# The last block of phase one multiplied plainly, attention work begun in the bursts, and more places for side work in the plain slices

## Chip, cores and metric

One Trainium2 chip, one of its cores. The metric is device time in microseconds (us) of one launch, lower is better. The engines are named as in the profile: PE (TensorE matmul), PEld (its weight loads), DVE (VectorE), ACT (ScalarE), POOL (GpSimd), SP (SyncE, which here only issues DMAs).

## What is computed

```python
# q, k, v: [8, 8, 576, 64]; attention inside chunks of 64 positions
scores = scale * np.matmul(q_c, k_c.transpose(0, 1, 2, 4, 3))
scores = scores - np.max(scores, axis=-1, keepdims=True)
attn = np.exp(scores)
attn = attn / (np.sum(attn, axis=-1, keepdims=True) + 1e-09)
x = (attn @ v_c) as [4608, 512]
x = ((x @ w_a) * (x @ w_b)) @ w_out             # phase one, d_ff 1536
h = ((x @ w1) * (x @ w2)) @ w3                  # phase two, d_ff 1024
out = h @ w_out2                                # [4608, 512]
```

The weights arrive as 64-bit floats and are turned into 32-bit ones on the chip. Each 32-bit operand of a large product is split into a high part and a remainder, and a product is three matmul passes (`SEQ`: high by low, low by high, high by high).

## The kernel before

The 4608 tokens are 9 blocks of 512. A phase (`ph` 0 or 1) goes through the `d_ff` columns in steps `f` of 128 (12 in phase one, 8 in phase two). In a step two first products `a` and `b` are made, multiplied into `g`, and `g` enters the second product, which sums over the steps in four PSUM tiles (`Second`, tiles `acc`, 3 matmuls to a part, 4 parts to a step).

Stages of a phase, in order:

- **Plain slices** (`plain_step`): blocks 0 and 1. Each step has a slice T=0 and a slice T=1; a slice is `first` twice, 12 matmuls each into `pa` and `pb`. The slices of T=0 run `AHEAD` (3) steps ahead of T=1. Only T=0 carries on to its second product; T=1 stores its `g` in the tiles `G`. Meanwhile weights are converted (`Pump`, `Conv`: about four DVE instructions, one of ACT and one of POOL for each) and, in phase one, the attention of the next blocks is computed (`Unit`, one for each block and pair of heads: `turn`, `scores` with `soft1`, `soft2`, `flip`, `apply` with `put`; on PE their tiles are `t`, `s`, `f`, `x`).
- **Burst** (`burst`): second product of the block whose `g` lie in `G`: 12 matmuls for each `f`, first the four parts that were still pending. `ready` makes a step's `gh` (ACT) and `gl` (POOL). The operands of the next two blocks are formed and split meanwhile (`strassen_pieces`: `minus` on DVE, then a cast on ACT and a subtraction on DVE, tiles `xP`).
- **Steps** (`block_steps`, `strassen_step`): two blocks at once by Strassen's scheme, seven products (`product`, tiles `P`) of 6 matmuls with 512 columns, combined by three copies on ACT and three additions on DVE (tiles `c`); `g` of one block goes to its second product, the other waits in `G` for the next burst.
- This pair of burst and steps comes four times in each phase. The fourth has one block alone, the ninth (`LONE`): Strassen inside the block, `single`, with 256 columns to a matmul. In phase one these steps also carry the conversion of the weights `w_out2` and `w3` (26 conversions), transposes of `w3` (`turn_w3`, tile `w3p`, then `w3t`) and eight products `w3 @ w_out2` (`fuse`, 24 matmuls each into `wf`), so that phase two multiplies by one fused matrix.

The order is written by hand (`manual_schedule`): every engine executes its instructions in program order. Side work lies in a `Track`, a list of pieces (cost, starts on PE or not, function). A step calls `point()` at set places; a point emits pieces until the share of cost emitted equals the share of points passed. A piece that starts on PE is emitted only as the first piece of a point (lines 59 to 71), and what is left at the end comes out at once in `finish`:

```python
while self.left and self.done < self.total * self.at / self.points:
    cost, needs, emit = self.left[0]
    if needs and not pe:
        return
```

DMAs of q, k and v are queued by `ask` and put on SP by `tick` (called by `first`, `product` and `Second.part`) or, where a unit needs them, by `settle`. Weight stores are queued by `store` and put on ACT's queue by the second `tick` after it. PSUM has eight banks: `rA` to `rD` for first products and side work, `acc0` to `acc3`. Attention uses `rB` and `rD`, `turn_w3` and `fuse` use `rD`.

Of the kernel before, what the change touches and what calls it, by code (L numbers as in the profile page):

```python
# [9 lines left out]
F32 = mybir.dt.float32  # L10
F32R = mybir.dt.float32r
# [67 lines left out]
def chunk_attention_two_gated_products(  # L79
# [158 lines left out]

    def split(dst_h, dst_l, src, eng_l):
        nc.scalar.copy(dst_h, src)  # L240
        eng_l.tensor_tensor(dst_l, src, dst_h, op=ALU.subtract)  # L241
# [10 lines left out]
    class Unit:  # L252
# [16 lines left out]
        def banks(self, name):  # L269
            return [bank("BD"[i], f"{name}{i}_{self.nm}") for i in range(2)]  # L270
# [149 lines left out]
    class TurnedOnPE(Unit):  # L420
# [47 lines left out]
        def flip_bank(self):  # L468
            return bank("D", f"f_{self.nm}")
# [79 lines left out]
    def strassen_pieces(x32, nm, single=False):  # L549
# [12 lines left out]

        def value(p, kt):
            name = f"x{p}{kt}{nm}"
            if p == "P1":
                return src(0, 0, kt)
            if p == "P2":
                return src(0, 1, kt)
            if p == "P3":
                return src(1, 1, kt)  # L570
            if p == "P5":
                diff["t1", kt] = minus(src(1, 0, kt), src(0, 0, kt), name)
                return diff["t1", kt]
            if p == "P6":
                diff["t2", kt] = minus(src(1, 1, kt), diff["t1", kt], name)
                return diff["t2", kt]
            if p == "P7":
                return minus(src(1, 1, kt), src(1, 0, kt), name)
            return minus(src(0, 1, kt), diff["t2", kt], name)
# [9 lines left out]
        def one(p, kt):  # L589
# [5 lines left out]
        order = ["P5", "P1", "P2", "P6", "P3", "P7", "P4"]  # L595
        return parts, [
            (1.4 if p in ("P5", "P6", "P7", "P4") else 0.7, False, lambda p=p, kt=kt: one(p, kt))
            for p in order
            for kt in range(2)
        ]  # L600

# [87 lines left out]
    def load_part(ph, f, i):  # L689
# [7 lines left out]
        pairs.setdefault((ph, f), {})[i] = t  # L697

# [121 lines left out]
    state = {"pending": None_()}  # L820
# [56 lines left out]
    def plain_step(ph, j, T, f, nm, point, gplaces, sums, tags):  # L877

        w = pairs[ph, f]
        xq = [quadrants[T, 0], quadrants[T, 1]]  # L880
# [11 lines left out]
        first(w, 1, xq, f"pb{nm}", pb)  # L892
        if T == 1:
            nc.vector.tensor_tensor(g_place(ph, f"{ph}p", f, gplaces), pb, sa, op=ALU.mult)
            del pairs[ph, f]
        else:
            nc.vector.tensor_tensor(sa, pb, sa, op=ALU.mult)
            pend.rest()
# [404 lines left out]
```

## Time and profile before

| | before |
|---|---|
| median of 3 runs | 1790.8 us (1788.63 to 1791.69) |
| profiled execution, own time | 1786.45 us |
| its span | 1784.6 us |
| busy share PE / PEld / DVE / ACT / POOL | 90% / 72% / 50% / 31% / 25% |
| granted TensorE clock, mean of the span | 0.963 of 2.4 GHz |

The span runs from the first to the last instruction of the profiled execution. A row of the timeline gives start, length, engine, line, operation, tile written and tiles read, count, and in brackets how long the engine was idle before and what ended that. A row of waits gives the waiting engine and tile, what it waited for, the sum in us, the number of times and the longest. A row of a window gives its length, each engine's busy time and number of instructions, the granted clock, the share of the 16 DMA engines and GB/s.

### The profile page before, as it was taken

The numbers are of one execution on the slowest core, as the hardware profiler recorded it, in microseconds if no ns is written. First come the engines' busy times: TensorE is split into PE (matmuls) and PEld (weight loads), VectorE is DVE, ScalarE is ACT, GpSimd is POOL, SyncE is SP. The second block draws the span as 40 slices with busy tenths as digits, with TensorE's granted clock in tenths as the row PEclk, the third lists the DMA queues.
The fourth block names the chain that finished last, engine by engine and source line by source line (L and its number), as shares of the span: only waits on it lengthen the run. The fifth ranks groups of instructions, "written<-read, shape, count | busy, mean of one in ns | idle before, by whom it ended". The sixth has DMA issues, their size and how long they took to land.

```text
span 1784.6 us, 24867 instructions
## 1 busy us (share of the span) xinstructions
PE 1609.8 (90%) x9232; PEld 1293.8 (72%) x9232; DVE 888.5 (50%) x1484; ACT 557.4 (31%) x1009; POOL 442.7 (25%) x354
## 2 busy tenths in 40 slices
PE   5769999699899999999998798889989989989998
PEld 3557777577677777777886676778768868868787
DVE  5748783476665655555224744355354442242231
ACT  4434443222224222322224322232332331231232
POOL 1304342111123221322123422222122222222232
PEclk8969999899999999999999899999999999999999
DMA  8757766676677887676566876596467756656674
GB/s 212 232 146 227 245 191 197 189 244 198 201 226 223 228 214 204 195 232 192 180 195 226 289 262 217 179 324 212 178 225 257 241 196 216 205 193 205 205 264 174
DMA packets 291703, 385.44 MB, mean 216 GB/s; under 512 B 174848, under 2 KB 195328, under 8 KB 291584
## 3 DMA queue, kind: packets, MB, share of 16 engines
q1 hardware_dynamic: 258656, 298.92, 55.1%
q10 hardware_dynamic: 32928, 84.95, 12.4%
q8 instruction: 73, 1.20, 0.3%
q14 instruction: 46, 0.38, 0.1%
HBM read 301.99 MB, written 81.79 MB: 215 GB/s over the span
## 4 chain that ended last, share of the span: by engine, by line
PE 62%; DVE 14%; DMA 8%; issue 5%; ACT 5%; POOL 2%; SPq 2%; ACTq 1%; POOLq 0%; DVEq 0%
PE P L756 32%; PE acc L785 16%; PE pb L742 5%; PE pa L742 4%; PE wf L988 3%; DVE xP L560 2%; SPq L148 2%; DVE xP L241 2%; DMA wo<-dwo 1%; DVE c L844 1%; ACT xP L240 1%; PE x L391 1%; DMA qk<-in_k_dram 1%; DMA x2d<-ev 1%; ACT ev L794 1%
## 5 line engine op out<-in xcount | busy, mean ns | idle before, releaser
L756 PE MATMUL P<-xP,w 128*128 128x512 f32 (+1 forms) x3360 | 735.8, 372 | 53.4 <-DVE c L844 30.7
L756 PEld LDWEIGHTS P<-xP,w 128*128 128x128 f32 x3360 | 584.3, 192 | 177.5 <-DVE c L844 40.9
L844 DVE TENSOR_TENSOR c<-P,c 128x512 f32<-128x512 f32 (+1 forms) x240 | 148.4, 621 | 350.0 <-PE P L756 338.0
L872 POOL TENSOR_TENSOR G<-c,c 128x512 f32<-128x512 f32 x60 | 78.2, 1303 | 517.0 <-DVE c L844 517.0
L841 ACT COPY c<-P 128x512 f32<-128x512 f32 (+1 forms) x240 | 127.3, 533 | 220.7 <-PE P L756 217.8
L785 PE MATMUL acc<-gh,wo 128*128 128x512 f32 x480 | 174.8, 402 | 0.0
L240 ACT CAST gh<-c 128x512 fp32r<-128x512 f32 x60 | 37.3, 621 | 333.1 <-DVE c L871 323.9
L742 PE MATMUL pb<-xq,w 128*128 128x512 f32 x480 | 124.3, 410 | 0.0
L742 PE MATMUL pa<-xq,w 128*128 128x512 f32 x480 | 121.5, 403 | 1.9 <-DVE w L645 1.9
L241 POOL TENSOR_TENSOR gl<-c,gh 128x512 fp32r<-128x512 f32 x60 | 78.2, 1304 | 162.2 <-ACT gh L240 162.2
L785 PE MATMUL acc<-wo,gh 128*128 128x512 f32 x320 | 112.2, 394 | 3.3 <-ACT gh L240 3.3
L742 PEld LDWEIGHTS pb<-xq,w 128*128 128x128 f32 x480 | 94.2, 199 | 20.9
L742 PEld LDWEIGHTS pa<-xq,w 128*128 128x128 f32 x480 | 91.5, 194 | 22.6 <-DVE w L645 2.3
L785 PEld LDWEIGHTS acc<-gh,wo 128*128 128x128 f32 x480 | 92.3, 192 | 19.9
L871 DVE TENSOR_TENSOR c<-P,c 128x512 f32<-128x512 f32 x60 | 41.5, 691 | 121.2 <-PE P L756 121.2
L785 PE MATMUL acc<-gl,wo 128*128 128x512 f32 x240 | 95.7, 399 | 0.0
L785 PEld LDWEIGHTS acc<-wo,gh 128*128 128x128 f32 x320 | 60.5, 189 | 16.9 <-ACT gh L240 4.1
L240 ACT CAST xP<-xP 128x512 fp32r<-128x512 f32 (+1 forms) x64 | 36.3, 567 | 113.7 <-DVE xP L560 113.7
L195 POOL TENSOR_TENSOR cv<-cv 128x512 f32<-128x512 f32 x38 | 45.3, 1191 | 99.9 <-DVE cv L189 75.0
L241 DVE TENSOR_TENSOR xP<-x,xP 128x512 fp32r<-128x512 f32 (+1 forms) x48 | 49.7, 1080 | 40.7 <-ACT xP L240 40.7
L241 DVE TENSOR_TENSOR xP<-xP,xP 128x512 fp32r<-128x512 f32 (+1 forms) x64 | 44.2, 691 | 43.8 <-ACT xP L240 43.8
L785 PE MATMUL acc<-wo,gl 128*128 128x512 f32 x160 | 63.6, 397 | 1.5 <-POOL gl L241 1.5
(132 smaller groups left out, 2158.8 us busy)
## 6 DMA issues: line engine op xcount, KB each, us to landing
w<-dw SPq DMA_DIRECT2D x200, 512.0 KB, 4.4
wo<-dwo SPq DMA_DIRECT2D x168, 512.0 KB, 4.3
dw<-w ACTq DMA_DIRECT2D x80, 512.0 KB, 4.1
w<-dw SPq DMA_DIRECT2D x80, 256.0 KB, 3.0
su<-d SPq DMA_DIRECT2D x20, 512.0 KB, 5.1
d<-cv ACTq DMA_DIRECT2D x38, 256.0 KB, 4.4
cv_o<-in_moe_w_out_dram SPq DMA_DIRECT2D x18, 512.0 KB, 5.5
x2d<-ev ACTq DMA_DIRECT2D x36, 256.0 KB, 3.6
```

The source lines that it names most:

```text
L148: nc.sync.dma_start(*asks["left"].popleft())
L195: eng.tensor_tensor(self.w, hi.bitcast(F32), lo, op=ALU.add)
L240: nc.scalar.copy(dst_h, src)
L241: eng_l.tensor_tensor(dst_l, src, dst_h, op=ALU.subtract)
L742: nc.tensor.matmul(ps, w[m][:, kk // 2, wp, kk % 2], xq[kk // 2][:, kk % 2, xp], start=(n == 0), stop=(n == 3 * KM - 1),)
L756: nc.tensor.matmul(ps, w[:, wp, kt], x[:, kt, xp], start=(begins and n == 0), stop=(n == 5), skip_group_check=True,)
L785: nc.tensor.matmul(acc[m], a, b, start=(f == 0 and (wp, gp) == SEQ[0]), stop=(f == NF[ph] - 1 and (wp, gp) == SEQ[-1]),)
L841: nc.scalar.copy(t, src)
L844: add = lambda o, a, b: nc.vector.tensor_tensor(o, a, b, op=ALU.add)
L871: nc.vector.tensor_tensor(g, last, c11, op=ALU.mult)
L872: nc.gpsimd.tensor_tensor(g_place(ph, nm.split("_")[0], f, gplaces), c22, c12, op=ALU.mult)
L988: nc.tensor.matmul(ps, t[:, gp, jj], wo2[jj // 2][:, jj % 2, wp], start=(jj == 0 and (wp, gp) == SEQ[0]), stop=(jj == NF[1] - 1 and (wp, g ...
```

## The change

Four edits, beside line shifts:

1. **The lone block of phase one.** `lone_steps` runs `plain_step` for it with the banks `rA` and `rC`: 24 matmuls of 512 columns for a step in place of 42 of 256. `lone_pieces` splits its four tiles in the burst ahead (4 pieces in place of 14). Its weights come by `load_plain`, two tiles of 512 KB for a step in place of four (three of 512 KB, one of 256 KB). Two loads of the conversions are issued before that burst, one behind it, in place of three behind it. The side work has 58 points in place of 81.
2. **Attention in the bursts.** `burst` takes the tracks `at` and calls their points from the fifth `f` on (8 points in each of the three bursts of phase one that have attention to come). There, scores and results use `acc2` and `acc3`.
3. **Forming ahead of splitting.** In `strassen_pieces` the DVE subtraction (`formed`) and the split (`one`) are pieces of their own, 22 of cost 0.7 with the same total; the differences of P5 and P6 are formed first.
4. **More points in a plain slice.** A T=0 slice has five points in place of three: the third pending part moves ahead of `pb`, with a point between, and a point stands between the product with `sa` and the last part. The totals of the tracks are set to match.

```diff
-        order = ["P5", "P1", "P2", "P6", "P3", "P7", "P4"]
+        order = [(formed, "P5"), (formed, "P6"), (one, "P5"), (one, "P1"), (one, "P2"),
+            (formed, "P7"), (one, "P6"), (formed, "P4"), (one, "P3"), (one, "P7"), (one, "P4")]
...
+    def lone_pieces(x32, nm):
+        xq = [pool.tile([P, 2, 2, NT], F32R, tag=f"xo{3 + K}", name=f"xl{K}{nm}") for K in range(2)]
...
+    def load_plain(ph, f, m):
+        t = w_tile(4 * (f % 2) + m, f"w{ph}_{f}_{m}")
+        nc.sync.dma_start(whole(t).bitcast(F32), dw[ph][f][m])
...
+        if freed:
+            freed(0)
         sa = tmp(f"sa{nm}")
         nc.scalar.copy(sa, pa)
         point()
         if T == 0:
             pend.part()
             pend.part()
+            point()
+            pend.part()
         point()
...
             nc.vector.tensor_tensor(sa, pb, sa, op=ALU.mult)
+            point()
             pend.rest()
...
             track.point()
+            if f > 3:
+                for a in at:
+                    a.point()
             s.rest()
...
-        late = Track(attention_pieces(U[NHP:]), 3 * AHEAD - 1)
+        late = Track(attention_pieces(U[NHP:]), 5 * AHEAD)
...
-                at = Track(attention_pieces(units), 3 * (len(order) - n) - 2)
+                at = Track(attention_pieces(units), 4 * (len(order) - n) - 2)
...
+        def lone_steps(ph, xq, at):
...
+                plain_step(ph, LONE, 0, f, f"{ph}L_{f}", point, None, sums, "AC", xq, freed)
...
-                    n_pts = PTS * steps
+                    n_pts = PTS * steps + steps - 4
...
+                if lone:
+                    pump.cap += 3 * NF[1]
+                    for i in range(2):
+                        pump.load(slot("G"))
+                burst(ph, j + 1, places, pieces, at, state.pop("ready", None))
...
-                    at.append(Track(track, PTS * steps - 3))
+                    at.append(Track(track, 5 * steps - 2))
```

Three places where instructions move. Names carry the block, the step and a running number.

ACT, end of the first three T=0 slices of phase one, before (`e`, `pT`, `xq` are the exponentials, transposed weights and results of attention, `sa_1_0` is the first slice of T=1, `dw` and `d` are weight stores):

```order
L478 COPY pT_2_1084<-f_2_1085 128x512
L240 CAST xq_1109<-x_1_2_1091 128x4x64
L240 CAST xq_1109<-x_1_2_1092 128x4x64
L357 ACTIVATE e_3_1133<-e_3_1133 128x512
L478 COPY pT_3_1144<-f_3_1145 128x512
L240 CAST xq_1109<-x_1_3_1157 128x4x64
L240 CAST xq_1109<-x_1_3_1158 128x4x64
L885 COPY sa_1_0_1198<-pa_1_0_1183 128x512
L463 COPY qT_0_1206<-t_2_0_1208 128x4x128
L463 COPY kT_0_1207<-t_2_0_1209 128x4x128
L157 DMA dw_3_0_76<-w_3_0_937 128x1024
L157 DMA d_0_3_147<-cv_3_0_786 128x512
```

The same place with the change:

```order
L670 CAST w_3_0_1013<-cv_3_0_818 128x2x256
L180 ACTIVATE cv_o_926<-cv_o_926 128x512
L242 CAST xq_1091<-x_1_2_1073 128x4x64
L242 CAST xq_1091<-x_1_2_1074 128x4x64
L362 ACTIVATE e_3_1131<-e_3_1131 128x512
L157 DMA dw_3_0_76<-w_3_0_1013 128x1024
L157 DMA d_0_3_147<-cv_3_0_818 128x512
L242 CAST gh_0_2_1148<-sa_0_2_1004 128x512
L483 COPY pT_3_1152<-f_3_1153 128x512
L242 CAST xq_1091<-x_1_3_1159 128x4x64
L242 CAST xq_1091<-x_1_3_1160 128x4x64
L913 COPY sa_1_0_1200<-pa_1_0_1185 128x512
```

The stores of conversion `3_0` stood behind the whole attention of heads 3 and behind `sa_1_0`; now they stand ahead of the last `pT`, and conversion and second-product work lies between the attention rows.

ACT, second burst of phase two, before (`ev` copies the finished sums out, `gh_3b` is what a step of the burst waits for):

```order
L240 CAST xP_12450<-xP_12451 128x512
L240 CAST xP_12450<-xP_12455 128x512
L240 CAST xP_12459<-x_4_0_11711 128x512
L794 COPY ev_2_0_12473<-acc_2_0_11845 128x512
L797 DMA out_dram<-ev_2_0_12473 128x512
L794 COPY ev_2_1_12479<-acc_2_1_11849 128x512
L797 DMA out_dram<-ev_2_1_12479 128x512
L794 COPY ev_2_2_12485<-acc_2_2_11853 128x512
L797 DMA out_dram<-ev_2_2_12485 128x512
L794 COPY ev_2_3_12491<-acc_2_3_11867 128x512
L797 DMA out_dram<-ev_2_3_12491 128x512
L240 CAST gh_3b_12494<-G_0_11771 128x512
```

With the change:

```order
L242 CAST xP_12036<-xP_12028 128x512
L820 COPY ev_2_0_12050<-acc_2_0_11423 128x512
L823 DMA out_dram<-ev_2_0_12050 128x512
L820 COPY ev_2_1_12056<-acc_2_1_11427 128x512
L823 DMA out_dram<-ev_2_1_12056 128x512
L820 COPY ev_2_2_12062<-acc_2_2_11431 128x512
L823 DMA out_dram<-ev_2_2_12062 128x512
L820 COPY ev_2_3_12068<-acc_2_3_11445 128x512
L823 DMA out_dram<-ev_2_3_12068 128x512
L242 CAST gh_3b_12071<-G_0_11349 128x512
```

Two of the three casts of `xP` that stood ahead of the copies now stand behind `gh_3b`.

DVE, a middle step of the lone block, before (`c` and `g` belong to the Strassen step, `cv_w` to a conversion, `wf` is the split of a fused product):

```order
L844 TENSOR_TENSOR c_4_9480<-P_4_9482,c_4_9480 128x256
L241 TENSOR_TENSOR w3t_9502<-w3p_0_9503,w3t_9502 128x512
L844 TENSOR_TENSOR c_4_9498<-P_4_9464,c_4_9498 128x256
L241 TENSOR_TENSOR wf_9542<-wf_9517,wf_9542 128x512
L179 TENSOR_SCALAR cv_w_2_1_9401<-cv_w_2_1_9401 128x512
L185 SCALAR_TENSOR_TENSOR cv_w_2_0_9355<-cv_w_2_0_9355 128x512
L188 TENSOR_SCALAR cv_w_2_0_9355<-cv_w_2_0_9355 128x512
L189 SCALAR_TENSOR_TENSOR cv_w_2_0_9355<-cv_w_2_0_9355 128x512
L844 TENSOR_TENSOR c_4_9471<-P_4_9473,c_4_9471 128x256
L241 TENSOR_TENSOR w3t_9502<-w3p_1_9570,w3t_9502 128x512
L867 TENSOR_TENSOR g_4_9588<-P_4_9473,c_4_9480 128x256
```

With the change:

```order
L243 TENSOR_TENSOR w3t_9311<-w3p_0_9312,w3t_9311 128x512
L243 TENSOR_TENSOR wf_9347<-wf_9322,wf_9347 128x512
L179 TENSOR_SCALAR cv_w_2_1_9245<-cv_w_2_1_9245 128x512
L185 SCALAR_TENSOR_TENSOR cv_w_2_0_9219<-cv_w_2_0_9219 128x512
L188 TENSOR_SCALAR cv_w_2_0_9219<-cv_w_2_0_9219 128x512
L189 SCALAR_TENSOR_TENSOR cv_w_2_0_9219<-cv_w_2_0_9219 128x512
L928 TENSOR_TENSOR sa0L_9303<-pb0L_9360,sa0L_9303 128x512
L243 TENSOR_TENSOR w3t_9311<-w3p_1_9376,w3t_9311 128x512
```

Between `wf` and the end of a step there was the step's own addition `c` and its product `g`; now there is one product, `sa0L`.

## Rows read from the trace of the kernel before

**Rows 1.** Page: busy time, share of the span and instructions of each engine.

```profile
PE 1609.8 (90%) x9232; PEld 1293.8 (72%) x9232; DVE 888.5 (50%) x1484; ACT 557.4 (31%) x1009; POOL 442.7 (25%) x354
```

**Rows 2.** Windows: plain slices (two), first burst, lone steps, a burst of phase two.

```profile
41.65:106.33 64.68, 43.56 (x405) 33.60 (x401) 40.72 (x76) 26.87 (x47) 18.05 (x14) 0.79 0.64 197
106.33:293.31 186.98, 172.41 (x1223) 137.57 (x1221) 121.19 (x204) 78.12 (x132) 58.78 (x45) 0.95 0.65 209
293.31:345.65 52.34, 40.02 (x157) 30.45 (x157) 27.21 (x34) 18.17 (x32) 13.92 (x10) 0.90 0.66 188
971.04:1166.07 195.03, 157.24 (x894) 135.74 (x893) 103.75 (x191) 57.37 (x113) 53.30 (x49) 0.94 0.68 240
1419.45:1455.03 35.58, 29.79 (x113) 22.70 (x112) 20.84 (x23) 15.77 (x28) 11.20 (x8) 0.90 0.57 183
```

**Rows 3.** Timeline of PE, undisturbed: plain slices, then lone steps of phase two.

```profile
1232.41 2.88 PE L742 MATMUL pa<-xq,w 128*128 128x512 f32 x12
1235.13 2.88 PE L742 MATMUL pb<-xq,w 128*128 128x512 f32 x12
...
1736.58 4.43 PE L756 MATMUL P<-xP,w 128*128 128x256 f32 x36
1740.85 0.39 PE L785 MATMUL acc<-wo,gh 128*128 128x512 f32 x1
```

**Rows 4.** Waits of PE in the lone steps of phase one.

```profile
PE P L756 <- DVE c L844: 13.5, 8, 4.2
PE P L756 <- ACT c L841: 12.7, 8, 4.7
```

**Rows 5.** Chain in order of time, lone steps of phase one: start, us, what.

```profile
1046.33 0.45 PE w3p L979 x4
1046.81 0.60 ACT w3t L240
1047.43 0.70 DVE w3t L241
```

**Rows 6.** Timeline of POOL, start of these lone steps: one of a run of conversions.

```profile
999.30 1.42 POOL L195 TENSOR_TENSOR cw_o<-cv_o 128x512 f32<-128x512 f32 x1 [2.40 <-DVE cv_o L189]
```

**Rows 7.** Timeline of PE, from the end of the third T=0 slice on.

```profile
85.20 0.69 PE L391 MATMUL x<-pT,v 64*64 64x64 f32 x32
...
103.35 1.08 PE L475 MATMUL f<-ident,e 128*128 128x128 f32 x4 [3.98 <-DVE e L365]
...
106.33 4.93 PE L742 MATMUL pa<-xq,w 128*128 128x512 f32 x12
...
123.19 1.08 PE L462 MATMUL t<-ident,qk 128*128 128x128 f32 x4 [4.72 <-DMA dwo<-wo]
```

**Rows 8.** Waits of SP from 84 to 132.

```profile
SPq L173 <- DMA d<-cv: 16.6, 1, 16.6
```

**Rows 9.** Groups of 41.65 to 293.31: attention on PE, and one reader of its banks.

```profile
L462 PE MATMUL t<-ident,qk 128*128 128x128 f32 x96 | 15.2, 305 | 11.0 <-DMA dwo<-wo 4.7 <-DMA v<-in_v_dram 2.8 <-PE pa L742 1.2
L463 ACT COPY kT<-t 128x512 f32<-128x512 f32 x12 | 13.5, 1129 | 3.8 <-PE t L462 3.8
L340 PE MATMUL s<-kT,qT 64*64 64x64 f32 x384 | 10.2, 233 | 9.1 <-DVE xq L241 3.8 <-ACT kT L463 3.1 <-ACT x L405 2.2
L391 PE MATMUL x<-pT,v 64*64 64x64 f32 x388 | 9.7, 240 | 5.3 <-ACT pT L478 5.3
L475 PE MATMUL f<-ident,e 128*128 128x128 f32 x48 | 8.3, 301 | 9.4 <-ACT kT L463 5.3 <-DVE e L365 4.1
```

**Rows 10.** Timeline of ACT and PE, second burst of phase two.

```profile
1425.00 0.62 ACT L240 CAST xP<-xP 128x512 fp32r<-128x512 f32 x1 [2.96 <-DVE xP L560]
...
1430.71 0.50 PE L785 MATMUL acc<-wo,gh_3b 128*128 128x512 f32 x1 [2.23 <-ACT gh_3b L240]
```

**Rows 11.** Waits of PE in the first burst of phase one.

```profile
PE acc L785 <- DMA wo<-dwo: 8.8, 1, 8.8
```

**Rows 12.** Groups of DVE, whole span: forming a difference of differences.

```profile
L560 DVE TENSOR_TENSOR xP<-x,xP 128x512 f32<-128x512 f32 x24 | 30.7, 1280 | 0.0
```

More of the change, by code (lines that the diff above doesn't have):

```diff
@@ L269, in banks @@
         def banks(self, name):
-            return [bank("BD"[i], f"{name}{i}_{self.nm}") for i in range(2)]
+            return [
+                psum.tile([P, NT], F32, tag=state["banks"][i], name=f"{name}{i}_{self.nm}")
+                for i in range(2)
+            ]
         def by_parity(self, t):
@@ L468, in flip_bank @@
         def flip_bank(self):
-            return bank("D", f"f_{self.nm}")
+            return psum.tile([P, NT], F32, tag=state["banks"][1], name=f"f_{self.nm}")
         def flip(self):
@@ L593, in one @@
             split(to[:, 0], to[:, 1], value(p, kt), nc.vector)
[L595 removed]
+        order = [
+            (formed, "P5"),
+            (formed, "P6"),
+            (one, "P5"),
+            (one, "P1"),
+            (one, "P2"),
+            (formed, "P7"),
+            (one, "P6"),
+            (formed, "P4"),
+            (one, "P3"),
+            (one, "P7"),
+            (one, "P4"),
+        ]
         return parts, [
[L597 to L600 removed]
+            (0.7, False, lambda do=do, p=p, kt=kt: do(p, kt)) for do, p in order for kt in range(2)
+        ]
+    def lone_pieces(x32, nm):
+        xq = [pool.tile([P, 2, 2, NT], F32R, tag=f"xo{3 + K}", name=f"xl{K}{nm}") for K in range(2)]
+        def one(kt):
+            to = xq[kt // 2][:, kt % 2]
+            split(to[:, 0], to[:, 1], x32[kt], nc.vector)
+        return xq, [(0.7, False, lambda kt=kt: one(kt)) for kt in range(KM)]
     dw = [
@@ L904, in ready, with burst @@
         return g_parts(gplaces[f // 4][:, f % 4], f"{ph}_{j}b{f}", nc.gpsimd)
-    def burst(ph, j, gplaces, others, first=None):
+    def burst(ph, j, gplaces, others, at, first=None):
         n = NF[ph]
         sums = []
+        state["banks"] = ("acc2", "acc3")
         track = Track(others, 2 * n // 3)
@@ L926, in burst @@
         track.finish()
-        state["pending"] = None_()
+        state["pending"], state["banks"] = None_(), ("rB", "rD")
     def attention_pieces(units):
@@ L1191, in chunk_attention_two_gated_products @@
                 state["outs"].ahead(2)
-                x, pieces = strassen_pieces(x32, f"{ph}{sb}", sb == NSB)
+                lone = ph == 0 and sb == NSB
+                if lone:
+                    x, pieces = lone_pieces(x32, f"{ph}{sb}")
+                else:
+                    x, pieces = strassen_pieces(x32, f"{ph}{sb}", sb == NSB)
                 if sb == 1:
@@ L1204, in chunk_attention_two_gated_products @@
                     attention_begins(units)
-                burst(ph, j + 1, places, pieces, state.pop("ready", None))
-                steps = NF[ph]
-                at = []
-                if ph == 0 and sb < NSB:
-                    n_pts = PTS * steps
+                    n_pts = PTS * steps + steps - 4
                     if sb == NSB - 1:
```

68 lines of the change are left out of this document (42 added, 26 removed).

## Prediction

> **What bounds the kernel now.** I read first the page's busy shares. TensorE is busy for 1609.8 of 1784.6 us, 90% [rows 1], so whatever the change gains comes out of the other 175 us, or out of stretches in which PE runs at a low granted clock, or out of PE's own work. Second, the windows by stage, to see where those are. The reader is to see that they are not spread evenly: the three first slices and the drain of attention behind them have PE busy for 43.56 of 64.68 us at a clock of 0.79, the lone steps for 157.24 of 195.03 at 0.94, the first burst for 40.02 of 52.34 [rows 2], and a burst of phase two for 29.79 of 35.58, at 0.90. The change touches all of these stages. Third, for each of them, PE's timeline and waits, to see which wait ends last. Prices at full clock come from undisturbed stretches: 12 matmuls of 512 columns start 2.72 us after the 12 ahead of them (1235.13 less 1232.41), 0.2267 us each; 36 of 256 columns take 4.27 us (1740.85 less 1736.58), 0.1186 each [rows 3].
>
> **The lone block, PE's own work.** Strassen's 42 matmuls a step are 504 in 12 steps, 504 x 0.1186 = 59.8 us. The plain ones are 24 a step, 288 x 0.2267 = 65.3. So PE's own work grows by 5.5 us. The rest stays: second products 144 x 0.2267 = 32.6, eight fused products of 24 matmuls 43.5, sixteen transposes at 0.45 [rows 5] 7.2. Own work is 143.1 before and 148.6 after. The stage takes 195.0 [rows 2], so 51.9 us are lost in it: 37.8 idle, and 14 of slow clock. The Trainium skill, "TensorE: Matmul & The Clock Gate", section "Back-to-back issue gap", gives the gap of one matmul as its columns over 2.4 plus 2.5 ns: 109.2 and 215.8 ns, by which the exchange would cost 7.2 us in place of 5.5 and the sum be 1.7 less of a gain, and so speaks against this edit a little more than the rows; its figure for a sustained stream, about 131 ns for 512 columns, is not what the rows show, and they decide.
>
> **The lone block, what is lost.** PE waits there 13.5 us for DVE's `c` and 12.7 us for ACT's `c`, in eight waits each of up to 4.7 us [rows 4]. These small combinations stand in DVE's and ACT's queues behind conversions and splits of `wf`, and Strassen's seven products of 0.71 us (6 x 0.1186) go through four banks: a late reader stops PE after some two of them. A plain step has one ACT copy and one DVE product, and PE has 2.7 us (one product) to 5.4 us of other work before it needs that bank again. So most of these waits go. What is late next: (a) the start. Its first eight conversions follow one another at 2.40 + 1.42 = 3.8 us on POOL [rows 6]; three to a step make 11.5 us, while a step without `wf` owns 5.4 + 2.7 = 8.2, so three steps lose some 10 us, the early loads notwithstanding. (b) Each of eight fused products waits for ACT's and DVE's part of the last `w3t`, 0.60 + 0.70 [rows 5], with one part of three matmuls (0.68) beside it: 0.62 x 8 = 5. (c) By estimate 3 for `gl`, 2 at the end, 3.5 of slow clock. That is 23.5 lost: 172, a term of **-23**. Ends: only some 8 lost (-38); the idle 37.8 stays and the clock gives back all but 3 (-6). I take the middle, as (a) and (b) rest on rows and the rest is small.
>
> **The plain slices of phase one.** The drain runs from 85.20 to 106.33 [rows 7], 21.1 us for eight attention pieces on PE. A piece there owns 0.90 (43.4 us busy over 48 pieces in four rows [rows 9]), 7.2 together, so 13.9 are lost to ACT's and DVE's turns, as the 3.98 before an `f` [rows 7]. With 15 points, and a slice's PE work between them, I expect two of these eight to be left: 21.1 x 2/8 less 1.8 own = 3.5 lost, and two new waits for a bank being read, 1.13 each [rows 9]: a gain of 8. Behind the drain PE waits 4.72 us for a weight [rows 7], because SP stood 16.6 us on a store of a converted weight [rows 8] that no `tick` issues during the drain, and the clock falls. In the changed order that store stands ahead of the last attention piece; I count 8 us for it (4.72, one more wait of about 1, and some 2 to 3 of slow clock). The rest of the slices idles 186.98 - 172.41 = 14.6 us [rows 2]; with thinner pieces, -3. Term **-19**, ends -38 (nearly all of the idle and slow clock) and 0 (the drain's waits reappear between the slices).
>
> **Bursts and steps of phase one.** The first burst's long wait is 8.8 us for a load of `wo` [rows 11]; it is a matter of DMA queues, which the edit doesn't shorten: **-2** (-8 to +4, the lower end if the wait vanishes). In the steps attention gets thinner, as some of it now lies in the bursts: **-2** (-6 to +4, two or three waits such as those of rows 9). The three later bursts of this phase: forming ahead of splitting against attention that enters `acc2` and `acc3` there, which second products don't use before the next steps: **-3** (-6 to +3).
>
> **Bursts of phase two.** In the second one ACT's cast of `xP` waits 2.96 us for DVE's difference, behind it come four copies `ev`, and then the cast `gh_3b` that PE waits for, 2.23 us [rows 10]; the burst idles 5.8 us and runs at 0.90 [rows 2]. After the change one cast stands ahead of the copies in place of three, and its difference has been formed. There are three such bursts with blocks still to come; this one takes 35.58 us [rows 2] against 24.5 of own work (96 matmuls x 0.2267 = 21.8, and 12 pending ones 2.7). Of these 11 us I expect 4 to 5 back in each, **-13**. Ends -24 (8 each) and 0. Plain slices of phase two get more points but little to put there: 0 (-4 to +3, one conversion earlier or later).
>
> **Sum.** -23 - 19 - 2 - 2 - 3 - 13 = -62. The profiled execution's own time was 1786.45, 4.3 us under the runs' median of 1790.8; its changed counterpart is 1724.4, and the median by the same distance **1729**.
>
> **The rivals.** *The lone steps stay paced by conversions* (chance 0.14). For it: DVE is busy 103.75 and POOL 53.30 us in this stage [rows 2], the conversions remain, and 58 points in place of 81 make each point's heap larger. Against: PE's waits are for Strassen's small combinations, not for converted weights. The term is -6 in place of -23: 1746.
>
> *The slices give nothing* (0.11): the drain's chain of ACT and DVE turns moves between the slices, and the store is held as long as before. For it: attention is the same work on the same two banks. Against: the store's place in the order. 1729 + 19 = 1748.
>
> *DVE and POOL block each other in the bursts* (0.05). Forming a difference of differences takes 1.28 us in the mean [rows 12], where a subtraction of the same size with an operand in PSUM takes 0.70 [rows 5]. Now four of these subtractions in a row come first in a burst, where POOL makes `gl`. If each were held for one POOL subtraction such as the 1.42 us of rows 6, up to 5.7 us in each burst, the gain in phase two's bursts would be gone: 1742. The Trainium skill has such a rule ("SBUF — State Buffer", section "Who interferes with whom": a DVE instruction with two SBUF inputs contends with a GpSimd one that reads SBUF, and who comes second waits in full); the row's 1.28 bears it out in part.
>
> *Slower: banks of attention* (0.07). The pieces `t`, `s`, `x`, `f` share two banks, and each reader must be done before the next piece writes. In the slices PE now idles 11.0 + 9.1 + 5.3 + 9.4 = 34.8 us before 48 pieces [rows 9], 0.73 each, since a product of 2.7 us usually lies between. More points in a slice put them behind one part of 0.68 us only. If each then waited for one to two readings of 1.13 us [rows 9], 1.7 to 2.26, the idle would be 82 to 108 and the slices cost 47 to 74 more, against 43 gained elsewhere: 1794 to 1821, about 1808. It decides at (34.8 + 43) / 48 = 1.6 us for each piece. Against it: the total of points is spread so that many points emit nothing.
>
> *The change doesn't do what it says* (0.05): attention and conversions end up where they were, and PE's 5.5 us eat the rest: within 0.2% of 1790.8.
>
> **How the numbers follow.** The forecast has 0.58. Faster by over 0.2% (3.6 us, about what a measurement of this kernel can tell from no change) are the forecast and the first three rivals, 0.88; same 0.05; slower 0.07. The terms' ends don't fall together: half of the good ends gives some 1700, and the first two rivals together, -25, with a little more, 1762. Left out are the last two rivals, 0.12, and the tails.
>
> **What would show it.** Right: the lone steps near 172 us, with PE's waits for `c` gone and waits on `wf`, `gl` or converted weights of a few us in their place; no drain over 6 us before the first slice of T=1, and SP's 16.6 us wait short; bursts of phase two near 31 us with no 2.96 us wait for `xP`; busy time of PE a few us higher or, by the better clock, lower. Wrong: lone steps over 185 us with DVE or POOL busy throughout; `t` and `s` waiting over 1.6 us each in the slices; the same wait for `gh` in phase two's bursts. If the time is above 1762, either two of the rivals hold together or the banks do.

## The result and the profile after

The changed kernel takes 1736.2 us in the median of four runs (1725.4 to 1738.3), against 1791.2 for the kernel before: a ratio of 0.967 with a 95% interval of 0.962 to 0.972. That is faster by 2.8 to 3.8%, and inside the range that was given; the forecast of 1729 was 7 us too low. The profiled execution took 1736.8 us, with a span of 1734.8, against 1786.45 and 1784.6: 49.8 us less of span, where the prediction's sum was 62. All times here are of fast executions; one run of a later kernel, 2124.1 us at a granted clock of 0.69, is left out of its median.

Windows of the changed kernel, in the order of [rows 2], with the same columns:

```profile
41.57:104.38 62.81, 45.68 (x404) 34.31 (x401) 39.72 (x76) 27.55 (x46) 17.46 (x14) 0.77 0.70 218
104.38:281.50 177.12, 167.69 (x1222) 134.55 (x1221) 123.53 (x205) 76.11 (x129) 55.55 (x44) 0.98 0.68 216
281.50:334.51 53.01, 42.67 (x191) 33.65 (x189) 30.80 (x46) 19.61 (x36) 16.18 (x11) 0.87 0.64 181
956.41:1139.23 182.82, 160.11 (x678) 126.12 (x677) 97.76 (x152) 52.98 (x89) 45.03 (x37) 0.94 0.57 202
1389.01:1416.03 27.02, 26.00 (x113) 20.67 (x111) 21.95 (x23) 15.57 (x28) 12.98 (x8) 1.00 0.69 227
```

The stretch to the first slice of T=1 is 1.9 us shorter, the slices behind it 9.9, the lone steps 12.2, the burst of phase two 8.6; the first burst is 0.7 longer. Set beside the terms of the sum, each stage taken from PE's first instruction in it to the next stage's first (us; the differences are taken before rounding; attention of the first block, the steps of phase two and what follows them differ by 0.3 at most):

| stage | before | after | difference | term |
|---|---|---|---|---|
| lone steps of phase one | 195.0 | 182.8 | -12.2 | -23 |
| slices of phase one | 251.7 | 239.9 | -11.7 | -19 |
| first burst | 52.3 | 53.0 | +0.7 | -2 |
| steps of phase one | 502.8 | 499.7 | -3.1 | -2 |
| bursts two to four of phase one | 122.6 | 122.2 | -0.4 | -3 |
| four bursts of phase two | 137.5 | 114.3 | -23.2 | -13 |
| plain slices of phase two | 119.1 | 119.1 | 0.0 | 0 |

Where the lone steps lose now, by PE's waits in them (waiting tile, what for, sum, times, longest):

```profile
PE acc L811 <- POOL gl0L L243: 14.6, 6, 3.2
PE acc L811 <- ACT gh0L L242: 5.2, 3, 4.1
PE wf L1026 <- DVE w3t L243: 2.1, 3, 0.7
```

The 26 us of waits for `c` [rows 4] are gone, and 20 us for the two halves of `g` stand in their place. POOL's timeline in the first of these steps says why:

```profile
969.56 1.42 POOL L195 TENSOR_TENSOR cw_o<-cv_o 128x512 f32<-128x512 f32 x1 [2.63 <-DVE cv_o L189]
970.94 1.26 POOL L243 TENSOR_TENSOR gl0L<-sa0L,gh0L 128x512 fp32r<-128x512 f32 x1
```

`gl0L` starts the moment a conversion's subtraction ends. That subtraction was emitted at the new point between the product `sa` and the last part, which stands ahead of the lines that make `gh` and `gl`; it waits 2.63 us for DVE's share of the conversion, with `gl` behind it in the queue. In all six waits a conversion's subtraction ends as `gl0L` starts. The waits for `gh` are another matter: 4.1 of their 5.2 us come in the second step, where DVE starts the product `sa` 3.8 us after PE has finished `pb`, behind a conversion, and ACT makes `gh` behind a conversion's cast.

Where in the stage the time is lost, by the windows of its first four, next five and last three steps:

```profile
956.41:1005.30 48.89, 35.97 (x142) 27.77 (x141) 36.52 (x56) 18.04 (x31) 18.10 (x14) 0.90 0.69 237
1005.30:1082.69 77.39, 75.14 (x343) 59.91 (x342) 38.34 (x60) 21.70 (x36) 17.07 (x16) 1.00 0.58 204
1082.69:1139.23 56.54, 49.00 (x198) 38.45 (x196) 22.90 (x36) 13.24 (x24) 9.85 (x9) 0.91 0.46 168
```

The slices, PE's timeline around the drain (compare [rows 7]):

```profile
96.88 0.40 PE L811 MATMUL acc<-gh,wo 128*128 128x512 f32 x1
101.46 1.09 PE L480 MATMUL f<-ident,e 128*128 128x128 f32 x4 [4.19 <-DVE e L370]
103.22 1.23 PE L396 MATMUL x<-pT,v 64*64 64x64 f32 x32 [0.68 <-ACT pT L483]
104.38 3.94 PE L768 MATMUL pa<-xq,w 128*128 128x512 f32 x12
...
122.68 1.99 PE L467 MATMUL t<-ident,qk 128*128 128x128 f32 x8 [5.04 <-DMA qk<-in_k_dram]
```

Two pieces are left for the drain, which takes 7 us in place of 21. But the third T=0 slice ends at 97.3 and not at 85.2. Windows of the three slices and of the drain, before and then after:

```profile
41.65:85.20 43.55, 33.96 (x228) 26.09 (x224) 29.86 (x53) 20.05 (x34) 15.29 (x12) 0.88 0.80 256
85.20:106.33 21.13, 9.60 (x178) 7.51 (x177) 10.86 (x24) 6.82 (x14) 2.76 (x2) 0.61 0.31 75
```
```profile
41.57:97.28 55.71, 43.44 (x368) 32.55 (x364) 36.49 (x71) 25.71 (x43) 16.19 (x13) 0.79 0.69 217
97.28:104.38 7.10, 2.25 (x36) 1.76 (x37) 3.23 (x6) 1.83 (x3) 1.26 (x1) 0.66 0.76 221
```

The slices are 12.2 us longer: PE idles 2.7 us more in them and is busy 9.5 us more, at a clock of 0.79 in place of 0.88. And the wait of about 5 us behind the drain is still there, for another transfer. SP's timeline and its longest wait tell which:

```profile
102.10 0.37 SPq L173 DMA_DIRECT2D cv<-in_moe_w_a_dram  x1
102.51 1.87 SPq L148 DMA_DIRECT2D qk<-in_q_dram  x3
117.64 0.37 SPq L173 DMA_DIRECT2D cv<-in_moe_w_b_dram  x1
118.06 0.58 SPq L148 DMA_DIRECT2D qk<-in_q_dram  x1
```
```profile
SPq L173 <- DMA d<-cv: 19.6, 4, 13.2
```

SP passes the load it was held at before (that store does go out earlier, at 98.3 on ACT's queue), stops 13.2 us at the next one, whose slot is freed by the next store (114.65), and the `k` that PE needs stands behind it.

The second burst of phase two, ACT's timeline (compare [rows 10]):

```profile
1390.98 0.61 ACT L242 CAST xP<-xP 128x512 fp32r<-128x512 f32 x1
1393.31 0.59 ACT L820 COPY ev<-acc 128x512 f32<-128x512 f32 x1 [1.72 <-PE acc L811]
...
1397.32 1.14 ACT L242 CAST gh_3b<-G 128x512 fp32r<-128x512 f32 x2 [0.41 <-ACT ev L820]
```

ACT now waits for PE before the first copy, where before it waited 2.96 us for DVE; `gh_3b` comes 8.3 us into the burst (10.6 before), and PE waits for it no more.

### The profile page after: what moved, and what is told of

Its sections match the earlier page's. It is cut to its first block, busy times and chain, and to the rows that moved or that the text cites. A ratio compares the mean times of both kernels' runs of the same rounds, so it can differ in the third digit from the quotient of the medians.

```text
span 1734.8 us, 24276 instructions
## 1 busy us (share of the span) xinstructions
PE 1595.5 (92%) x9016; PEld 1275.7 (74%) x9016; DVE 874.5 (50%) x1430; ACT 548.5 (32%) x975; POOL 444.7 (26%) x342
## 4 chain that ended last, share of the span: by engine, by line
PE 71%; DVE 11%; DMA 7%; issue 4%; ACT 3%; POOL 2%; SPq 2%; ACTq 0%; POOLq 0%; DVEq 0%
PE P L782 34%; PE acc L811 18%; PE pb L768 6%; PE pa L768 5%; PE wf L1026 3%; DMA wo<-dwo 2%; DVE xP L243 2%; SPq L148 2%; PE pb0L L768 2%; PE x L396 1%; DVE c L870 1%; DMA qk<-in_q_dram 1%; PE t L467 1%; DMA v<-in_v_dram 1%; DMA cv_w<-in_moe_w_dram 1%
## 5 line engine op out<-in xcount | busy, mean ns | idle before, releaser
L782 PE MATMUL P<-xP,w 128*128 128x512 f32 (+1 forms) x2856 | 655.6, 382 | 24.5 <-DVE c L870 18.3
L782 PEld LDWEIGHTS P<-xP,w 128*128 128x128 f32 x2856 | 512.2, 188 | 140.2 <-DVE c L870 23.8
L870 DVE TENSOR_TENSOR c<-P,c 128x512 f32<-128x512 f32 (+1 forms) x204 | 133.7, 658 | 325.2 <-PE P L782 316.5
L867 ACT COPY c<-P 128x512 f32<-128x512 f32 (+1 forms) x204 | 114.5, 562 | 207.2 <-PE P L782 204.8
L811 PE MATMUL acc<-gh,wo 128*128 128x512 f32 x384 | 139.3, 400 | 0.0
L768 PE MATMUL pb<-xq,w 128*128 128x512 f32 x480 | 120.1, 400 | 0.0
L811 PEld LDWEIGHTS acc<-gh,wo 128*128 128x128 f32 x384 | 72.6, 189 | 16.4
L811 PE MATMUL acc<-gl,wo 128*128 128x512 f32 x192 | 75.7, 394 | 0.0
L820 ACT COPY ev<-acc 128x512 f32<-128x512 f32 x72 | 42.3, 587 | 95.9 <-PE acc L811 81.7
L362 ACT ACTIVATE e<-e 128x512 f32<-128x512 f32 x36 | 22.8, 632 | 100.0 <-DVE e L356 100.0
```

Of the source, the lines that this page charges most:

```text
L768: nc.tensor.matmul(ps, w[m][:, kk // 2, wp, kk % 2], xq[kk // 2][:, kk % 2, xp], start=(n == 0), stop=(n == 3 * KM - 1),)
L782: nc.tensor.matmul(ps, w[:, wp, kt], x[:, kt, xp], start=(begins and n == 0), stop=(n == 5), skip_group_check=True,)
L811: nc.tensor.matmul(acc[m], a, b, start=(f == 0 and (wp, gp) == SEQ[0]), stop=(f == NF[ph] - 1 and (wp, gp) == SEQ[-1]),)
L820: nc.scalar.copy(t, acc[m])
L867: nc.scalar.copy(t, src)
L870: add = lambda o, a, b: nc.vector.tensor_tensor(o, a, b, op=ALU.add)
```

## Experiments

Times are medians; ratios are to the kernel before, run on the same chip beside each group. "Stage" times are from the profile of the run. Between kernels whose order is the same up to a stage, that stage's time differs by 2 to 5 us (the slices of phase one take 237.2 to 241.9 us in seven such kernels), and the first steps of phase one, where they hold the same instructions, by 10, so smaller differences prove nothing. No later run was set beside the changed kernel itself: where the interval of a run overlaps its 0.962 to 0.972, a gain is shown by the stage and its waits and not by the whole.

**Part 1 undone.**

```diff
-                lone = ph == 0 and sb == NSB
+                lone = False
...
-                    at.append(Track(track, 5 * steps - 2))
+                    at.append(Track(track, PTS * steps - 3))
```

> The changed kernel with part 1 undone: the lone block of phase one by Strassen's scheme again, with its four loads, the 81 points and all loads of the conversions behind the burst. The two traces put 12.2 us of the gain in this stage (195.0 before, 182.8 after). If that is this part's own doing, the stage goes back to 193 to 197 us, PE waits there 10 us or more for c again, the bursts of phase two stay near 27 us, and the whole is about 12 us slower than the changed kernel: 1745. Rival: the stage gains because of what another part brings into it (weights converted earlier, the side work's points), or its loss is the conversions' own; then it stays within 3 us of 182.8.

1746.3 us, 0.975 [0.973, 0.978]. Window of the lone steps, and PE's waits in them:

```profile
950.10:1145.83 195.73, 157.99 (x893) 136.51 (x892) 104.14 (x191) 57.62 (x113) 53.24 (x49) 0.92 0.68 240
```
```profile
PE P L782 <- DVE c L870: 13.6, 8, 4.1
PE P L782 <- ACT c L867: 12.6, 9, 3.8
```

The stage is back at 195.7 and the waits for `c` at 26 us, so the gain in the lone steps needs this part. Part 4 enters it too, since the lone block runs `plain_step` with the new points; a lone block with three points was not run.

**Part 4 undone in the slices.**

```diff
         if T == 0:
             pend.part()
             pend.part()
-            point()
-            pend.part()
+            if freed:
+                point()
+                pend.part()
...
-        late = Track(attention_pieces(U[NHP:]), 5 * AHEAD)
+        late = Track(attention_pieces(U[NHP:]), 3 * AHEAD - 1)
...
```

> The changed kernel with part 4 undone in the two-block slices of both phases: three points in a slice of T=0 and the totals of before, while the lone block keeps five. The traces put 1.9 us of the gain ahead of the first slice of T=1 and 9.9 behind it. If the points make them, both go: slices of phase one 249 to 254 us in place of 239.9, the drain of 21 us is back, the whole near 1745. Rival: the 9.9 us are where a store and a load happen to meet (SP's queue), not the points' doing in itself; then only some of it comes back, the whole within 5 us of the changed kernel.

1747.1 us, 0.975 [0.972, 0.977]. Windows to the first slice of T=1 and behind it, to be read with the two of the changed kernel:

```profile
41.46:109.61 68.15, 46.39 (x405) 35.69 (x401) 40.58 (x76) 27.20 (x46) 18.10 (x14) 0.75 0.62 188
109.61:296.07 186.46, 171.21 (x1222) 136.85 (x1220) 121.25 (x204) 78.14 (x132) 58.62 (x45) 0.96 0.65 209
```

Both halves of the gain go, 5.3 and 9.3 us. The points make them.

**Three points in the first three slices alone**, five from the fourth on.

```diff
+        more = not (ph == 0 and f < AHEAD and j == 0)
...
-            point()
-            pend.part()
+            if more:
+                point()
+                pend.part()
...
```

> The changed kernel with three points in each of the first three slices, as before, and five from the fourth T=0 slice on. It tells apart where the slices' gain comes from. If from the drain (two pieces in place of eight at its end, and what lies behind it), the stretch from the first slice on takes 68 us to the first slice of T=1 and 184 to 187 behind it, as with three points throughout. If from the steady slices, the second part stays at 175 to 179.

1746.9 us in one run; its windows:

```profile
41.78:113.02 71.24, 46.36 (x405) 35.65 (x401) 40.57 (x76) 27.19 (x46) 18.07 (x14) 0.74 0.58 179
113.02:291.60 178.58, 168.48 (x1222) 135.48 (x1220) 122.73 (x205) 75.80 (x129) 55.81 (x44) 0.97 0.69 220
```

The second stretch stays at 178.6: its gain is the steady slices' own, not an effect of the drain. The first stretch takes 64.7, 68.2 and 71.2 us in the three kernels with three points, and 61.1 to 63.8 in ten of the eleven with five (64.7 in the other). So against the changed kernel's 62.8 us three points cost 1.9, 5.3 and 8.4 us there; the pair before and after showed the least of these.

**Part 3 undone.**

```diff
...
-            (0.7, False, lambda do=do, p=p, kt=kt: do(p, kt)) for do, p in order for kt in range(2)
+            (1.4 if p in ("P5", "P6", "P7", "P4") else 0.7, False, lambda p=p, kt=kt: both(p, kt))
+            for p in order
+            for kt in range(2)
```

> The changed kernel with part 3 undone: each difference is formed and split in one piece, in the order P5 P1 P2 P6 P3 P7 P4. The traces put 23 us in the four bursts of phase two (37.1, 35.6, 35.5, 29.3 before, 33.5, 27.0, 27.2, 26.7 after). If forming ahead makes them, the second and third go back to 34 to 37 us with PE waiting over 2 us for gh_3b and half the clock behind it, and the whole is 17 to 23 us slower than the changed kernel: 1750 to 1756. In phase one's bursts the theory expects less than 2 us each. Rival: the burst of phase two gains from something else, such as loads that come sooner; then it stays under 30.

1762.2 us, 0.984 [0.982, 0.986]. The second burst of phase two, window and PE's first wait:

```profile
1396.53:1431.89 35.36, 29.71 (x112) 22.58 (x111) 20.55 (x23) 15.77 (x28) 11.21 (x8) 0.90 0.56 184
```
```profile
PE acc L806 <- ACT gh_3b L242: 3.2, 3, 2.0
```

As expected in phase two (37.1, 35.4, 35.8 and 29.3 us). The whole is slower than expected, 1762.2 against 1750 to 1756, because of phase one: the three bursts with attention take 56.8, 46.6 and 45.1 us against 53.0, 42.0 and 42.7, so this part holds some 10 us there too (the first steps behind are 3 us shorter, within their spread), which the table above hides, since attention in the bursts costs as well.

**Is it the wait, or the number of casts?** First try, joined pieces with P1 and P2 in front (the edit against the run with part 3 undone):

```diff
-        order = ["P5", "P1", "P2", "P6", "P3", "P7", "P4"]
+        order = ["P1", "P2", "P5", "P6", "P3", "P7", "P4"]
```

> The changed kernel with each difference formed and split in one piece again, but in the order P1 P2 P5 P6 P3 P7 P4. In phase two's second burst as many casts of xP stand ahead of the four copies ev as before (three), but none of them waits for a difference. If the casts' wait for DVE was what made gh_3b late, bursts two and three take 26 to 29 us as in the changed kernel. If the number of casts ahead of the copies was it, they take 33 to 36 as before.

1768.2 us in one run, the second burst 37.0 us. This told nothing: five pieces come at the first point, not three, and the fifth is a cast of P5 that waits again,

```profile
1406.77 0.62 ACT L242 CAST xP<-xP 128x512 fp32r<-128x512 f32 x1 [2.92 <-DVE xP L565]
```

so the run has more casts and the wait as well. The second try keeps forming and splitting apart:

```diff
         order = [
+            (one, "P1"),
+            (one, "P2"),
             (formed, "P5"),
             (formed, "P6"),
             (one, "P5"),
-            (one, "P1"),
-            (one, "P2"),
```

> The changed kernel with the order P1 P2 ahead of the formed differences, each still a piece of its own. In phase two's second and third burst four casts of xP now stand ahead of the copies ev (one in the changed kernel, three before), and none of them waits for a difference; the run before it could not tell, since a fifth cast stood there that did wait. If the wait for a difference was what made gh_3b late, the bursts stay at 27 to 28 us. If the number of casts ahead of the copies was it, 30 to 36.

1728.0 us in one run. ACT's timeline in the second burst of phase two:

```profile
1383.88 2.18 ACT L242 CAST xP<-x 128x512 fp32r<-128x512 f32 x4
1386.22 0.59 ACT L820 COPY ev<-acc 128x512 f32<-128x512 f32 x1 [0.16 <-PE acc L811]
...
1390.22 1.14 ACT L242 CAST gh_3b<-G 128x512 fp32r<-128x512 f32 x2 [0.41 <-ACT ev L820]
```

Four casts stand ahead of the copies, end 0.16 us before PE has the first sum, and the burst takes 26.6 us, the third 26.7. The number was not it; a cast that waits for DVE was. This order also shows a price of the change's own: in the first burst of phase one PE waits 3.1 us for `gh_1b` in the changed kernel (0.9 before) and not at all here, and the burst takes 47.5 us in place of 53.0. That is one trace, and it was not tried with the edits below.

**Part 2 undone.**

```diff
-            if f > 3:
-                for a in at:
-                    a.point()
...
```

> The changed kernel with part 2 undone: no attention in the bursts, the tracks' totals as before. The traces show bursts 2 and 3 of phase one unchanged (41.5 and 42.9 before, 42.0 and 42.7 after), the two first step stages unchanged, and the third, whose attention has half the points, 3.7 us shorter. If that is this part's doing, the third goes back to 155 to 156 us and the whole is 2 to 5 us slower than the changed kernel, 1735 to 1738. Rival: attention in the burst costs as much as it saves; then the sum of bursts and steps of phase one stays within 2 us.

1732.9 us, 0.968 [0.966, 0.971], against 0.967 for the whole change. Bursts two and three are 39.1 and 40.7 us (42.0 and 42.7 with attention), the third steps 155.7 (151.9). The sum of bursts and steps of phase one is 676.6 us (674.9), so the rival holds by its own measure: attention in the bursts costs about what it saves. The 3.3 us by which the whole is shorter come from elsewhere (the lone steps take 179.2 us here, though this part does not touch them). This part has no gain that can be shown.

**`gh` and `gl` ahead of the point, in the lone block.**

```diff
             nc.vector.tensor_tensor(sa, pb, sa, op=ALU.mult)
+            g = g_parts(sa, nm, nc.gpsimd) if freed else None
             point()
             pend.rest()
...
-            state["pending"] = Second(ph, j, f, wo, g_parts(sa, nm, nc.gpsimd), sums)
+            state["pending"] = Second(ph, j, f, wo, g or g_parts(sa, nm, nc.gpsimd), sums)
```

> The changed kernel, in the lone block of phase one alone: gh and gl of a step are made straight behind the product sa, ahead of the point that stands between sa and the last part. In the changed kernel PE waits there 14.6 us for gl and 5.2 for gh, each time that a conversion's POOL subtraction stands just ahead of gl (six of twelve steps). If POOL's and DVE's queue order is the cause, PE's waits for gl fall under 4 us, half-clock stretches get fewer, and the stage takes 168 to 175 us in place of 182.8; the whole near 1723 to 1728. Rival: the stage is paced by the conversions themselves; then the wait appears elsewhere (w3p on cw_w, wf on wo, or the product sa late on DVE), and the stage stays over 179 us.

1727.4 us, 0.965 [0.963, 0.968]. Windows of the lone steps, of their first four and of their last three, and PE's waits:

```profile
955.18:1129.51 174.33, 158.45 (x678) 124.58 (x677) 91.11 (x148) 50.60 (x87) 45.01 (x37) 0.96 0.59 207
955.18:1003.78 48.60, 39.02 (x141) 29.66 (x141) 37.28 (x56) 17.76 (x31) 18.61 (x14) 0.86 0.70 240
1081.49:1129.51 48.02, 44.24 (x198) 34.97 (x196) 19.22 (x32) 12.12 (x22) 9.88 (x9) 1.00 0.50 179
```
```profile
PE acc L811 <- ACT gh0L L242: 4.7, 3, 2.4
PE acc L811 <- POOL gl0L L243: 3.1, 3, 1.2
...
PE w3p L1018 <- POOL cw_w L195: 1.8, 1, 1.8
```

The waits for `gl` fall from 14.6 to 3.1 us and the stage to 174.3: queue order on POOL was the cause of those waits. But all of the gain lies in the last three steps, 48.0 us in place of 56.5, at a clock of 1.00 in place of 0.91. The first four, in which the conversions crowd, take 48.6 against 48.9: PE idles 9.6 us in place of 12.9 and runs at 0.86 in place of 0.90, the waits for `gh` stay (4.7 us in place of 5.2), and 1.8 us for a converted weight come in place. So the rival isn't ruled out for these four steps; for the stage as a whole it is. The stage now ends with a new wait of 2.9 us for phase two's operands, and phase two's plain slices take 122.0 us in place of 119.1.

**Loads of q, k, v ahead of the next weights.**

```diff
                 attention_begins(units)
+                settle(asks["all"])
```

> The changed kernel with one line added: behind the drain, all loads of q, k, v for the next two units are put on SP at once, ahead of the loads of the next weights to convert. In the changed kernel SP stands 13.2 us on such a load until the store of that slot's old content is done, and PE waits 5.0 us for qk behind it, at half the clock. If that order is the cause, the 5.0 us wait goes and the slices of phase one get 5 to 9 us shorter (177.1 us from the first slice of T=1 on becomes 168 to 172). Rival: the converted weights, now loaded later, become what PE waits for; then the stretch stays within 3 us of 177.

1724.6 us, 0.964 [0.961, 0.966]. Window behind the first slice of T=1, and SP's timeline there:

```profile
104.22:271.62 167.40, 165.52 (x1222) 133.83 (x1220) 122.13 (x205) 75.58 (x129) 55.77 (x44) 0.99 0.73 231
```
```profile
101.85 2.56 SPq L148 DMA_DIRECT2D qk<-in_k_dram  x4
...
119.67 0.37 SPq L173 DMA_DIRECT2D cv<-in_moe_w_b_dram  x1
```

The first unit's `k` goes out at 101.85. SP still stands before the same kind of load (until 119.67), but PE no longer waits for what is behind it, and idles 1.9 us in the whole stretch, which is 9.7 us shorter.

**Both small edits; then with part 2 undone; then `gl` ahead in every slice.** The second is the first with the diff of part 2 undone, the third drops `if freed else None`.

> The changed kernel with both small edits of the runs before: in the lone block gh and gl straight behind the product, and the loads of q, k, v put on SP at once behind the drain. They gained 8.5 us in the lone steps and 9.7 in the slices. If these are separate places, both are kept: lone steps 173 to 176, slices behind the first slice of T=1 166 to 169, the whole 1714 to 1722. Rival: one lengthens what the other shortened, and the whole stays at 1724 or above.

1720.7 us, 0.962 [0.959, 0.964]:

```profile
102.49:272.63 170.14, 166.71 (x1222) 134.27 (x1220) 121.81 (x205) 75.61 (x129) 55.94 (x44) 0.98 0.71 228
947.58:1120.81 173.23, 156.63 (x677) 123.05 (x677) 90.96 (x148) 50.56 (x87) 45.00 (x37) 0.97 0.60 209
```

Both gains are kept (7.0 us in the slices, 1.1 short of the range that was expected, and 9.6 in the lone steps), though the slices of phase two take 121.9 in place of 119.1. This is the fastest kernel of the study.

> The kernel with both small edits, and part 2 of the change undone: no attention in the bursts. Alone, undoing part 2 made bursts 2 and 3 of phase one 3.0 and 2.1 us shorter and the third steps 3.8 longer. If that is an even exchange, this run lies within 3 us of the one with both edits. Rival: part 2 is worth having once the rest is tighter, and this run is over 4 us slower.

1725.6 us, 0.965 [0.962, 0.967]: 5.0 us slower, over the rival's 4, but the intervals overlap, and 3.3 us the other way came out of the first test of part 2. The sum of bursts and steps of phase one was shorter with attention inside in both tests, by 1.7 and 3.1 us, which is within the spread. Whether attention belongs in the bursts stays open.

> The kernel with both small edits and part 2 undone, and gh and gl made straight behind the product in every plain slice, not in the lone block alone. In the slices the second product of a step comes a whole slice of T=1 after gl, so nothing should wait for it: theory, the slices within 2 us, the whole within 3 us of the run without it. Rival: gl on POOL ahead of a conversion delays converted weights that the next slice needs, and the slices get over 3 us longer.

1726.7 us, 0.964 [0.962, 0.967]: the whole is within 3 us of the run before it, as expected. The slices are not within 2: those of phase one take 236.0 us in place of 230.2, the rival's sign, and those of phase two 119.7 in place of 124.4, where PE's waits of 1.9 us for `gh` and 0.6 for `gl` are gone. So something did wait for them, and the two differences cancel; with one trace of each, what makes the first isn't settled.

## Why the prediction was right, and where it was not

**What bounded the kernel** was read rightly: every part that was forecast to gain much did so by PE idle or half-clocked time. PE's idle time in the span fell by 35.5 us, its busy time from 1609.8 to 1595.5 although its own work grew. The sum of -62 came as near to the -49.8 as it did partly by luck: the lone steps and the slices gave 18 us less than counted, the bursts of phase two 10 more.

**Lone steps, -23 forecast, -12.2 measured.** The exchange of waits was right: the waits for `c` went, and came back with part 1 undone. By the prediction's working the stage loses 182.8 less 148.6, 34.2 us, where it counted 23.5: 22.7 idle (20 counted) and 11.5 in which PE is busy beyond its own work (3.5 counted). (a) held: in the first four steps PE idles 12.9 us, for some 10. (b) was too dear: 2.1 us measured for 5, as three of eight fused products waited. The step that failed is (c), "By estimate 3 for `gl`, 2 at the end, 3.5 of slow clock". In the last three steps alone `gl` cost 6.7 us, because the added point lets a conversion onto POOL ahead of `gl`. I had counted what a point spreads, and not which of the step's own instructions it is put ahead of. And the clock was 0.91 around these waits and 0.90 around those of (a), where 3.5 us of slow clock had been counted in all: that is the greater part of what was missed (not all of the 11.5 is clock: the five middle steps, at 1.00, are busy 2.6 us beyond the same working). With `gh` and `gl` put ahead the stage took 174.3, near the forecast's 172, but by another sum: 15.9 idle and 9.9 of extra busy time. PE's own 5.5 us were not isolated; PE is busy for 160.1 us against 158.0 with part 1 undone, both with some half clock in them. So between 5.5 and the 7.1 (the prediction has 7.2) that follow from the Trainium skill's page "TensorE: Matmul & The Clock Gate", section "Back-to-back issue gap", no stage here decides.

**Slices, -19 forecast, -11.7 measured.** "I expect two of these eight to be left" was right, and the drain lost 5.3 us over the two pieces' own work in place of 13.9. The other six were to cost "two new waits for a bank being read, 1.13 each". They made the slices 12.2 us longer, 6.8 more than their own 5.4: PE's idle time grew by 2.7 us, about as counted, but PE's busy time grew by 4.1 beyond the pieces' own, at a clock of 0.79 in place of 0.88, which the term had at nothing. So the stretch gained 1.9 us and not 8 (5.3 against part 4 undone). The step "I count 8 us" for SP's wait failed outright: the store moved, as the order said, and SP went on to the next load whose store had not moved, with the same 5 us for PE. What the forecast lacked was the load after the one that was freed. One line that puts q, k and v ahead of it gave the 8 us that I had counted (9.7, and 7.0 beside the other edit). The -3 for the rest of the slices was too small: with three points in the first slices, and PE's wait of 5.8 us for `k` still there, the stretch behind them gained 8.4 us. That the term came within its ends is in part luck: the steady slices made up half of what the other two counts missed.

**Bursts of phase two, -13 forecast, -23.2 measured.** The mechanism was right, the size was not. In the burst shown, PE's waits and the half-clock stretch both went, and it runs at 1.00 with 1.0 us idle: 8.6 us and not 4 to 5. Of these 8.6 us 4.8 are idle time and 3.8 PE's busy time, which had been at a clock of 0.90. I had not counted the clock's share, nor the fourth burst (-2.7). The rival of DVE and POOL did not decide, although its condition came true (below).

**Bursts of phase one, -5 together, +0.3 measured.** Forming ahead gains some 10 us there (part 3 undone); attention costs 5 in two of them (part 2 undone), and the rest of the difference lies within the spread. I saw neither size. In the first burst the wait for `wo` fell from 8.8 to 4.6 us, since attention fills it (8.9 with part 2 undone), and waits of 3.1 for `gh_1b` and 1.8 for attention's `kT` took its place.

**The slower rival** (banks of attention) didn't occur: behind the first slice of T=1 PE idles 9.4 us in 177.1, less than the 14.6 of before.

## What to carry to other kernels

A new place for side work is a place in every in-order queue: list which of the step's own instructions now stand behind it, above all those that feed the next matmul, and put them ahead. When a transfer held back by a store is freed, look at the next one in the same queue before counting the gain; put what PE needs next ahead of both. And a wait of some us that PE has to sit out can cost twice, once as its idle time and once more at the lower clock behind it (4.8 and 3.8 us in the second burst of phase two); the single waits of 0.7 us in the middle of the lone steps cost no clock, which stays at 1.00 there.

## What was not expected of the hardware

In the changed bursts, four differences are formed in a row on DVE, with POOL's `gl` beside the later ones. DVE's timeline in the second burst of phase two, then POOL's:

```profile
1389.82 1.28 DVE L565 TENSOR_TENSOR xP<-x,x 128x512 f32<-128x512 f32 x2
1391.02 1.78 DVE L565 TENSOR_TENSOR xP<-x,xP 128x512 f32<-128x512 f32 x1
1392.72 1.79 DVE L565 TENSOR_TENSOR xP<-x,xP 128x512 f32<-128x512 f32 x1
```
```profile
1390.70 1.55 POOL L243 TENSOR_TENSOR gl<-c,gh 128x512 fp32r<-128x512 f32 x1 [2.86 <-ACT gh L242]
1392.21 1.75 POOL L243 TENSOR_TENSOR gl_3b<-G,gh_3b 128x512 fp32r<-128x512 f32 x1
```

Two subtractions take 1.28 us together while POOL is idle for most of it, and two of the same size 3.49 us, from 1391.02 to 1394.51, while POOL subtracts beside them; POOL's own rise from 1.29 where DVE is idle to 1.55 and 1.75. The ends come in turn: DVE 1391.10, POOL 1392.25, DVE 1392.80, POOL 1393.95, DVE 1394.51. POOL ends 1.15 us after DVE each time and DVE 0.55 after POOL, a little less than each takes alone (1.29 and 0.64): so in these rows the second waits until the first has ended. This is what the Trainium skill's page "SBUF — State Buffer", section "Who interferes with whom", says of a DVE instruction with two SBUF inputs beside a GpSimd one that reads SBUF, and these rows agree with it. The rival of the prediction had all four held, up to 5.7 us in a burst; two of them were, for 2.2 us. The loss stays off PE's path: PE idles 1.0 us in this burst.

The other surprise is the spread: one of the changed kernel's four runs took 1725.4 us and the rest 1735.6 to 1738.3, and the first steps of phase one, with the same instructions in them, took 179.1 to 188.9 us over ten of the kernels shown here. What makes it is not known.
